# Moving the first normalisations of three groups to GpSimd in a two-stage transformer block on one core

## The chip, the cores and the metric

The kernel runs on one core of a Trainium2 chip. The number that counts is the device time of one launch in microseconds (us). The engines of the core, each with its own in-order stream of instructions, are PE (TensorE, the matrix engine; PEld is its loading of weights), DVE (VectorE), ACT (ScalarE), POOL (GpSimd) and SP (SyncE, which here issues nearly all transfers). An engine waits for others by semaphores, and everything that stands behind a waiting instruction on the same engine waits with it.

## The reference

The input x has 2048 rows of 512 channels, in bf16. Two residual steps follow each other; both are modulated by a vector c:

```python
mod = (_silu(c) @ w_mod).reshape(c.shape[0], 6, 1, -1)    # sa, ca, ga, sb, cb, gb
h = _layernorm(x, axis=-1) * (1 + ca) + sa
x = x + ga * _A_ref(h, A_wqkv, A_wo)
h = _layernorm(x, axis=-1) * (1 + cb) + sb
x = x + gb * _B_ref(h, B_w_gate, B_w_up, B_w_down)
```

`_A_ref` is an attention with 32 heads of 16 channels. Every row looks at 8 rows only: itself and those 2, 4, ... 14 rows before it. `_B_ref` is a gated feed-forward: gelu(h @ w_gate) * (h @ w_up), 1792 wide, times w_down.

## The kernel before

The rows are worked on in four groups of 512 (group 0 to 3), each laid out as 4 chunks of 128 rows. For one group the steps are these, with the lines of the kernel before:

- LN1: mean and variance of every row (DVE, L430 and L431, and for some chunks ACT, L408 to L419), then the inverse root as a power of -1/2 on POOL (`rst`, L471), then the normalised rows xn, one instruction per chunk of 128x512 (`norm_x`, L448, on DVE).
- xn is transposed so that channels lie on the partitions. This is done by PE as 16 small matmuls with the identity matrix for the names in `BY_PE` (`transp`, L484), and by one transposing DMA from SP for the others (L490). Four instructions (128x512 each) then multiply by 1 + ca and add sa (`transp_ev`, L522, on ACT) and leave hT. Group 0 has a path of its own (`transp0`, L507, and L538 and L540), in two halves.
- q, k and v: 12 tiles of 4 matmuls (L593), each copied out of PSUM by ACT (L613, L615, L619). v goes through DRAM (L625) and is read back four times, shifted (L634).
- The logits: DVE multiplies q by 8 shifted copies of k, four instructions pq of 128x4096 (L654), and PE sums over channels (LTp, L668). The softmax is on DVE and ACT (L680 to L712). Its weights go back to rows by PE and ACT (group 0, L726 and L735) or through DRAM (L740, L748).
- DVE multiplies by the shifted v, four instructions pv of 128x4096 (L761), PE sums (o_ps, L775), ACT copies (oT, L786), PE multiplies by wo (x_ps, L796), DVE adds x (L805).
- LN2, its transposition, then the feed-forward (g_ps and u_ps L829, gelu L863, copy L870, product L881, y_ps L841 and L853) and the stores.

The modulation vectors are products of w_mod with silu(c). The first two (sa and ca) are needed before any hT: `ldwm01` loads their 1024 columns in two halves of 256 rows (L245), `mods` multiplies them (L349), and DVE adds the 1 (L355). The blocks 2 to 5 of w_mod are loaded by L238 into two buffers in turn, so the third of these loads waits until PE has used the first. Blocks 2 and 5 become ga and gb (gR, L369), which scale wo and w_down (L391, L386). Blocks 3 and 4 become sb and 1 + cb (modT, L306).

The order of the work is written out. Every step is a generator of operations, called a thread, and the list `ORDER` holds the number of the thread whose next operation is issued. An engine gets its instructions in the order in which they are issued. Threads 0 to 29 are constants, loads, modulation and warm-up matmuls; group g has the 26 threads from 30 + 26g on. Nothing is decided at run time: a late operand makes the engine wait, and it does not take other work meanwhile.

Of the kernel before, what the change touches and what calls it, by code (L numbers as in the profile page):

```python
# [9 lines left out]
ALU = mybir.AluOpType  # L10
# [96 lines left out]
def kernel(  # L107
# [14 lines left out]
    P = 128  # L122
# [27 lines left out]
    def T(k, shape, dt, name):  # L150
        return pools[k].tile(shape, dt, name=name, tag=k)
# [69 lines left out]
    def loads():  # L221
# [5 lines left out]
        def ldx(sg, c0=0, c1=CPS, q=nc.sync):  # L227
            def f():
                if ("x", sg) not in B:
                    B["x", sg] = T("x", [P, CPS, D], BF16, "x")  # L230
                q.dma_start(out=B["x", sg][:, c0:c1, :],  # L231
                            in_=A_x[0, sg * SG:(sg + 1) * SG, :].rearrange("(p c) d -> p c d", p=P)[:, c0:c1, :])
            return f
# [8 lines left out]
        def ldwm01(h):  # L242
            if h == 0:
                B["wm01"] = T("prod", [P, 4, 2 * D], BF16, "wm01")
            nc.sync.dma_start(out=B["wm01"][:, 2 * h:2 * h + 2, :],  # L245
                              in_=w_mod[2 * h * P:(2 * h + 2) * P, 0:2 * D].rearrange("(t p) n -> p t n", p=P))

        def ldc():
            nc.sync.dma_start(out=c4[:], in_=c.rearrange("o (t p) -> (o t) p", p=P))
# [24 lines left out]
        def act_q():  # L274
            yield Op("ACT", 0.46, ldx(0, 2, 4, nc.scalar), fire="x0.2", lat=mb(0.25), dma=True)
        qs = [act_q()]
        def head_q():
            yield Op("SP", 0.47, ldx(0, 0, 2), fire="x0.0", lat=mb(0.25))
            yield Op("SP", 0.45, ldc, fire="c", lat=0.0)
            for h in range(2):  # L280
                yield Op("SP", 0.5, lambda h=h: ldwm01(h), take=[] if h else [SL["prod"]], fire=f"wm01.{h}", lat=mb(0.5))
# [45 lines left out]
    def mods():  # L327
# [15 lines left out]
        for h in range(2):  # L343
            def f(h=h):
                if h == 0:
                    B["mp01"] = T("mm", [P, 8], F32, "modT_ps")
                for ch in range(8):
                    for kt in (2 * h, 2 * h + 1):
                        nc.tensor.matmul(B["mp01"][:, ch:ch + 1], lhsT=B["wm01"][:, kt, ch * P:(ch + 1) * P],  # L349
                                         rhs=scT[:, kt:kt + 1], start=(ch == 0 and kt == 0), stop=(ch == 7 and kt == 3))  # L350
            yield Op("PE", 0.43, f, after=[f"wm01.{h}", "scT", "w15"], take=[] if h else [SL["mm"]],
                     give=[SL["prod"]] if h else [], fire=f"mp01.{h}")
# [3 lines left out]
        yield Op("DVE", 0.1, f, after=["mp01.1", "ident"], give=[SL["mm"]], fire="mod01")  # L356
# [81 lines left out]

    def norm_x(key, src, ev, parts=((0, 4),)):
        aa, ab = ACT_CH.get(ev, (0, 0))  # L440
        dv = [c4 for c4 in range(CPS) if not aa <= c4 < ab]
        for c4 in range(CPS):
            def f(c4=c4):
                k = norm_tiles(ev)
                if c4 == 0:
                    B[key] = T("xn", [P, CPS, D], BF16, "xn")
                m, o = (k["mv"][:, c4, 0:1], ALU.subtract) if c4 in dv else (k["s"][:, 1, c4:c4 + 1], ALU.add)
                nc.vector.tensor_scalar(out=B[key][:, c4, :], in0=src()[:, c4, :], scalar1=m,  # L448
                                        scalar2=k["rstd"][:, c4:c4 + 1], op0=o, op1=ALU.mult)
            yield Op("DVE", 0.325, f, after=[f"{ev}.rs{max(a for a, b in parts if a <= c4)}"],  # L450
                     take=[SL["xn"]] if c4 == 0 else [], fire=f"{ev}.x{c4}")
# [44 lines left out]
    BY_PE = ("LN1.1", "LN1.2", "LN2.0")  # L496
# [15 lines left out]
    def transp_ev(key, dkey, dtag, sc, bi, ev, dep):  # L512
        pe = ev in BY_PE
        for dtp in range(2):
            for dd in range(2):
                dt = 2 * dtp + dd

                def f(dt=dt, dtp=dtp, dd=dd):
                    if pe and dt == 0:
                        B[dkey] = T(dtag, [P, CPS, DT, P], BF16, dtag)  # L520
                    o = B[dkey][:, :, dt, :]
                    nc.scalar.activation(out=o, in_=B[key, dtp][:, :, dd, :] if pe else o, func=ACT.Identity,  # L522
                                         scale=sc(dt), bias=bi(dt))
                yield Op("ACT", 0.67 if pe else 0.71, f, after=[f"{ev}.t{dtp}" if pe else f"{ev}.t"] + dep,
# [437 lines left out]
```

## Time and profile before

Three runs took 237.4, 238.49 and 238.78 us; the median is 238.49. The profiled execution took 238.96 us, of which the profile covers a span of 237.1 us.

| what | us |
|---|---|
| profiled execution / its span | 238.96 / 237.1 |
| PE busy | 230.0 |
| DVE busy | 170.2 |
| ACT busy | 154.0 |
| POOL busy | 12.5 |
| PE idle from 12 us to 30 us of the span | 0.69 |
| PE idle from 30 us to 234 us | 0.75 |

All times in the text are counted from the start of the span. A row of the timeline has the start, the duration, the engine, the line, the operation and the tiles. A row of the chain of waits has the start and the duration of a piece of the work that ended last. A row of the groups has the busy time of all instructions of a kind and the mean of one in ns.

### The profile page before, as it was taken

The page shows a single profiled execution, that of the slowest core. Times are in us where ns is not written, and L with a number is a line of the kernel's source. Part 1 is how long each engine was busy: PE and PEld are TensorE (multiplying, and loading weights), DVE is VectorE, ACT ScalarE, POOL GpSimd, SP SyncE. Part 2 cuts the span into 40 slices and gives each one's busy share as a digit, 9 for nine tenths or more (in the row PEclk, how much of TensorE's full clock was granted, in tenths as well). Part 3 has the DMA queues.
Part 4 walks back from the last instruction along what each step waited for, and adds up shares of the span by engine and source line. Part 5 has one row for each costly group of instructions (what it writes and reads, how often), then busy time and mean ns, then how long its engine had stood idle before and what let it go on. Part 6 is the DMA issues. An engine that isn't in the chain of part 4 may idle for free.

```text
span 237.1 us, 3691 instructions
## 1 busy us (share of the span) xinstructions
PE 230.0 (97%) x1389; PEld 109.3 (46%) x1401; DVE 170.2 (72%) x238; ACT 154.0 (65%) x290; POOL 12.5 (5%) x39
## 2 busy tenths in 40 slices
PE   7798999999999999999999999999999999999995
PEld 2554555544554444444444444444444444444443
DVE  3799998999997999999997998978622202322222
ACT  4699999889798766947557962262679740266400
POOL 2510101000100000100000001000100000000000
PEclk9999999999999999999999999999999999999999
DMA  5999799999987529644105853810030001100011
GB/s 158 376 308 283 191 199 252 321 302 298 198 198 204 179 58 199 107 82 124 42 0 118 154 140 62 113 44 22 19 73 0 0 0 47 44 0 0 0 47 44
DMA packets 33417, 29.68 MB, mean 125 GB/s; under 512 B 12792, under 2 KB 30712, under 8 KB 33400
## 3 DMA queue, kind: packets, MB, share of 16 engines
q1 hardware_dynamic: 33256, 29.19, 50.2%
q10 hardware_dynamic: 144, 0.26, 0.4%
q8 instruction: 11, 0.18, 0.3%
q14 instruction: 6, 0.05, 0.1%
HBM read 22.37 MB, written 4.98 MB: 115 GB/s over the span
## 4 chain that ended last, share of the span: by engine, by line
PE 86%; DMA 8%; SPq 3%; ACT 1%; issue 1%; DVE 0%
PE g_ps L829 21%; PE u_ps L829 20%; PE y_ps L841 19%; PE qkv_ps L593 11%; PE x_ps L796 6%; DMA wm<-in_w_mod_dram 5%; DMA hT<-xn 3%; PE LTp L668 3%; PE o_ps L775 2%; SPq L223 1%; PE y_ps L853 1%; ACT hT L522 1%; PE hTp L484 1%; SPq L231 1%; PE modT_ps L306 0%
## 5 line engine op out<-in xcount | busy, mean ns | idle before, releaser
L829 PE MATMUL g_ps<-h,Wg 128*128 128x512 bf16 x224 | 57.4, 379 | 0.0
L829 PE MATMUL u_ps<-h,Wu 128*128 128x512 bf16 x224 | 57.3, 379 | 0.0
L863 ACT ACTIVATE gl<-g_ps 128x512 bf16<-128x512 f32 x56 | 33.5, 598 | 27.0 <-PE g_ps L829 27.0
L841 PE MATMUL y_ps<-Wd,hht 128*128 128x512 bf16 x203 | 45.6, 379 | 0.5 <-issue 0.2
L881 DVE TENSOR_TENSOR hht<-gl,ub 128x512 bf16<-128x512 bf16 x56 | 23.0, 421 | 31.8 <-ACT ub L870 31.7
L593 PE MATMUL qkv_ps<-hT,wqkv 128*128 128x512 bf16 x184 | 41.8, 380 | 0.5 <-ACT kT L615 0.4
L870 ACT CAST ub<-u_ps 128x512 bf16<-128x512 f32 x56 | 32.8, 586 | 14.4 <-PE u_ps L829 14.4
L654 DVE TENSOR_TENSOR pq<-qT,kT 128x4096 bf16<-128x4096 bf16 x16 | 36.1, 2285 | 0.2
L761 DVE TENSOR_TENSOR pv<-PT,V 128x4096 bf16<-128x4096 bf16 x16 | 35.8, 2284 | 0.1
L829 PEld LDWEIGHTS <-Wu 128*128 128x128 bf16 x224 | 21.8, 98 | 26.7 <-issue 0.8
L829 PEld LDWEIGHTS <-Wg 128*128 128x128 bf16 x224 | 21.6, 98 | 27.1 <-issue 1.7
L841 PEld LDWEIGHTS <-hht 128*128 128x128 bf16 x210 | 20.5, 98 | 25.0 <-issue 0.4
L593 PEld LDWEIGHTS <-wqkv 128*128 128x128 bf16 x184 | 20.2, 114 | 19.9 <-issue 2.8
L888 DVE TENSOR_TENSOR ot<-y_ps,x 128x512 bf16<-128x512 f32 x15 | 10.2, 689 | 20.1 <-PE y_ps L841 18.8
L471 POOL TENSOR_TENSOR rstd<-rstd,neghalf 128x4 f32<-128x4 f32 (+1 forms) x9 | 8.7, 966 | 154.8 <-DVE rstd L465 83.8
L522 ACT ACTIVATE h<-h,modT,scl 128x512 bf16<-128x512 bf16 x12 | 9.0, 805 | 11.8 <-DMA h<-xn 11.8
L796 PE MATMUL x_ps<-woP,oT 128*128 128x512 bf16 x60 | 15.3, 379 | 0.2
L430 DVE BATCH_NORM_STATS2 st<-x 128x6 f32<-128x512 bf16 x18 | 12.3, 686 | 3.5 <-DMA x<-in_A_x_dram 3.1
L786 ACT CAST oT<-o_ps 128x512 bf16<-128x512 f32 x16 | 8.6, 585 | 3.6 <-PE o_ps L775 3.6
L805 DVE TENSOR_TENSOR x<-x_ps,x 128x512 bf16<-128x512 f32 x16 | 10.7, 677 | 0.3 <-PE x_ps L796 0.2
L408 ACT ACTIVATE gl<-x 128x512 bf16<-128x512 bf16 x14 | 8.7, 630 | 2.9 <-DVE x L805 2.0
L796 PEld LDWEIGHTS <-oT 128*128 128x128 bf16 x64 | 7.2, 114 | 6.9 <-issue 0.4
(83 smaller groups left out, 183.2 us busy)
## 6 DMA issues: line engine op xcount, KB each, us to landing
V<-vscr SPq DMA_DIRECT2D x12, 520.0 KB, 8.5
wm<-in_w_mod_dram SPq DMA_DIRECT2D x6, 512.0 KB, 6.7
vscr<-vT SPq DMA_DIRECT2D x4, 512.0 KB, 6.3
out_dram<-ot SPq DMA_DIRECT2D x15, 128.0 KB, 1.7
Wu<-in_B_w_up_dram SPq DMA_DIRECT2D x1, 1792.0 KB
Wg<-in_B_w_gate_dram SPq DMA_DIRECT2D x1, 1792.0 KB, 9.5
wqkv<-in_A_wqkv_dram SPq DMA_DIRECT2D x3, 512.0 KB, 9.2
x<-in_A_x_dram SPq DMA_DIRECT2D x3, 512.0 KB, 9.5
```

The lines of the kernel that those rows point to most:

```text
L430: nc.vector.bn_stats(out=st[:], in_=src()[:, c4, :])
L522: nc.scalar.activation(out=o, in_=B[key, dtp][:, :, dd, :] if pe else o, func=ACT.Identity, scale=sc(dt), bias=bi(dt))
L593: nc.tensor.matmul(ps[:], lhsT=wqkv[blk][:, dt, j::4], rhs=B["hT", sg][:, :, dt, :], start=(dt == 0), stop=(dt == DT - 1))
L654: nc.vector.tensor_tensor(out=pq[:], in0=_ap(B["qT", sg][:, j, :], [[0, W], [1, SG]]), in1=_ap(kT[:, j, sg * SG + 2:sg * SG + 2 + SG], [[2 ...
L761: nc.vector.tensor_tensor(out=t[:], in0=_ap(B["PT", sg][:, 0, :], [[SG, 2], [0, 4], [1, SG]]), in1=_ap(v[:, 0, j, :], [[8, 2], [4 * (SG + ...
L796: nc.tensor.matmul(ps[:], lhsT=B["oT", sg][:, j, c4::CPS], rhs=woP[:, j, :], start=(j == 0), stop=(j == 3))
L805: nc.vector.tensor_tensor(out=x[:, c4, :], in0=B["x1ps", sg, c4][:], in1=x[:, c4, :], op=ALU.add)
L829: nc.tensor.matmul(ps[:], lhsT=Wt[:, dt, ft * P:(ft + 1) * P], rhs=B["h2T", sg][:, :, dt, :], start=(dt == 0), stop=(dt == DT - 1))
L841: nc.tensor.matmul(ps[:], lhsT=B["hh", sg, ft][:, c4 * P:(c4 + 1) * P], rhs=B["Wd", ft // 4][:, ft % 4, :], start=(ft == 0), stop=(ft == F ...
L863: nc.scalar.activation(out=gl[:], in_=B["g", sg, ft][:], func=ACT.Gelu_apprx_tanh)
L870: nc.scalar.copy(out=ub[:], in_=B["u", sg, ft][:])
L881: nc.vector.tensor_tensor(out=hh[:], in0=B["gl", sg, ft][:], in1=B["ub", sg, ft][:], op=ALU.mult)
```

## The change

- The normalised rows of LN1 of groups 1, 2 and 3 (12 instructions of 128x512) are written by POOL and not by DVE (`X_POOL`).
- LN1 of group 2 is transposed by a DMA and no longer by PE; that of group 3 was already. Their scaling and shifting (8 instructions of 128x512) is done by POOL in place of ACT (`H_POOL`).
- The loads of sa and ca are one block of 512 columns each, ca first, so rows of 1 KB in place of 2 KB. The matmuls follow block by block.
- Both halves of the first x come from SP, and the small vector c from ACT's queue; before, the second half of x came from ACT's queue and c from SP.
- `ORDER` is a new list. On PE the mods of block 3 move into the q, k, v matmuls of group 0, block 2 stands between the two transpositions of group 1 and block 4 behind them. On SP the transposing DMA of group 2 stands between the store of group 0's v and its four loads back. On DVE all four products pq of group 1 stand ahead of the four pv of group 0; before, two of them stood behind.

```diff
 ORDER = [
-    0, 0, 23, 23, 23, 23, 23, 23, 23, 23, 23, 23, 23, 2, 32, 2, 1, 22, 32, 32, 32, 32, 32, 22, 30, 30, 30, 32,
...
+    23, 1, 22, 0, 0, 23, 23, 23, 23, 2, 32, 2, 32, 23, 23, 22, 22, 24, 32, 32, 2, 2, 23, 23, 23, 23, 3, 30, 30,
...
-        def ldwm01(h):
-            if h == 0:
-                B["wm01"] = T("prod", [P, 4, 2 * D], BF16, "wm01")
-            nc.sync.dma_start(out=B["wm01"][:, 2 * h:2 * h + 2, :],
-                              in_=w_mod[2 * h * P:(2 * h + 2) * P, 0:2 * D].rearrange("(t p) n -> p t n", p=P))
+        def ldwm01(b):
+            if "wm01" not in B:
+                B["wm01"] = T("prod", [P, 4, 2, D], BF16, "wm01")
+            nc.sync.dma_start(out=B["wm01"][:, :, b, :], in_=w_mod[:, b * D:(b + 1) * D].rearrange("(t p) n -> p t n", p=P))
 
         def ldc():
-            nc.sync.dma_start(out=c4[:], in_=c.rearrange("o (t p) -> (o t) p", p=P))
+            nc.scalar.dma_start(out=c4[:], in_=c.rearrange("o (t p) -> (o t) p", p=P))
...
-        def act_q():
-            yield Op("ACT", 0.46, ldx(0, 2, 4, nc.scalar), fire="x0.2", lat=mb(0.25), dma=True)
-        qs = [act_q()]
+        qs = [one("ACT", 0.45, ldc, fire="c", lat=0.0, dma=True)]
         def head_q():
-            yield Op("SP", 0.47, ldx(0, 0, 2), fire="x0.0", lat=mb(0.25))
-            yield Op("SP", 0.45, ldc, fire="c", lat=0.0)
-            for h in range(2):
-                yield Op("SP", 0.5, lambda h=h: ldwm01(h), take=[] if h else [SL["prod"]], fire=f"wm01.{h}", lat=mb(0.5))
+            for c0 in (0, 2):
+                yield Op("SP", 0.47, ldx(0, c0, c0 + 2), fire=f"x0.{c0}", lat=mb(0.25))
+            for b in (1, 0):
+                yield Op("SP", 0.5, lambda b=b: ldwm01(b), take=[SL["prod"]] if b else [], fire=f"wm{b}", lat=mb(0.5))
...
+    X_POOL = ('LN1.1', 'LN1.2', 'LN1.3')
+
     def norm_x(key, src, ev, parts=((0, 4),)):
         aa, ab = ACT_CH.get(ev, (0, 0))
         dv = [c4 for c4 in range(CPS) if not aa <= c4 < ab]
+        eng, ve, w = ("POOL", nc.gpsimd, 0.75) if ev in X_POOL else ("DVE", nc.vector, 0.325)
...
-                nc.vector.tensor_scalar(out=B[key][:, c4, :], in0=src()[:, c4, :], scalar1=m,
+                ve.tensor_scalar(out=B[key][:, c4, :], in0=src()[:, c4, :], scalar1=m,
                                         scalar2=k["rstd"][:, c4:c4 + 1], op0=o, op1=ALU.mult)
-            yield Op("DVE", 0.325, f, after=[f"{ev}.rs{max(a for a, b in parts if a <= c4)}"],
+            yield Op(eng, w, f, after=[f"{ev}.rs{max(a for a, b in parts if a <= c4)}"],
...
-    BY_PE = ("LN1.1", "LN1.2", "LN2.0")
+    BY_PE = ('LN1.1', 'LN2.0')
+
+    H_POOL = ('LN1.2', 'LN1.3')
...
-                    nc.scalar.activation(out=o, in_=B[key, dtp][:, :, dd, :] if pe else o, func=ACT.Identity,
-                                         scale=sc(dt), bias=bi(dt))
+                    if ev in H_POOL:
+                        nc.gpsimd.tensor_scalar(out=o, in0=o, scalar1=sc(dt), scalar2=bi(dt), op0=ALU.mult, op1=ALU.add)
+                    else:
+                        nc.scalar.activation(out=o, in_=B[key, dtp][:, :, dd, :] if pe else o, func=ACT.Identity,
+                                             scale=sc(dt), bias=bi(dt))
```

More of the change, by code (lines that the diff above doesn't have):

```diff
@@ L225, in loads, with ldx @@
         B["x", 0] = T("x", [P, CPS, D], BF16, "x")
-        def ldx(sg, c0=0, c1=CPS, q=nc.sync):
+        def ldx(sg, c0=0, c1=CPS):
             def f():
@@ L230, in f @@
                     B["x", sg] = T("x", [P, CPS, D], BF16, "x")
-                q.dma_start(out=B["x", sg][:, c0:c1, :],
+                nc.sync.dma_start(out=B["x", sg][:, c0:c1, :],
                             in_=A_x[0, sg * SG:(sg + 1) * SG, :].rearrange("(p c) d -> p c d", p=P)[:, c0:c1, :])
@@ L341, in mods, with f @@
                  act="exp", fire="pre")
-        for h in range(2):
-            def f(h=h):
-                if h == 0:
+        for b in (1, 0):
+            def f(b=b):
+                if b:
                     B["mp01"] = T("mm", [P, 8], F32, "modT_ps")
[L347 to L352, printed above, removed]
+                for ch in range(4):
+                    for kt in range(4):
+                        nc.tensor.matmul(B["mp01"][:, 4 * b + ch:4 * b + ch + 1],
+                                         lhsT=B["wm01"][:, kt, b, ch * P:(ch + 1) * P], rhs=scT[:, kt:kt + 1],
+                                         start=(kt == 0), stop=(kt == 3))
+            yield Op("PE", 0.43, f, after=[f"wm{b}", "scT", "w15"], take=[SL["mm"]] if b else [],
+                     give=[] if b else [SL["prod"]], fire=f"mp{b}")
         def f():
             nc.vector.tensor_tensor(out=mod01[:], in0=B["mp01"][:], in1=c01[:], op=ALU.add)
-        yield Op("DVE", 0.1, f, after=["mp01.1", "ident"], give=[SL["mm"]], fire="mod01")
+        yield Op("DVE", 0.1, f, after=["mp0", "ident"], give=[SL["mm"]], fire="mod01")
     def mods_g(k):
@@ L521, in f @@
                     o = B[dkey][:, :, dt, :]
-                    nc.scalar.activation(out=o, in_=B[key, dtp][:, :, dd, :] if pe else o, func=ACT.Identity,
-                                         scale=sc(dt), bias=bi(dt))
-                yield Op("ACT", 0.67 if pe else 0.71, f, after=[f"{ev}.t{dtp}" if pe else f"{ev}.t"] + dep,
+                    if ev in H_POOL:
[3 more added lines that the diff above has]
+                                             scale=sc(dt), bias=bi(dt))
+                yield Op("POOL" if ev in H_POOL else "ACT", 0.75 if ev in H_POOL else 0.67 if pe else 0.71, f, after=[f"{ev}.t{dtp}" if pe else f"{ev}.t"] + dep,
                          take=[SL[dtag]] if pe and dt == 0 else [],
```

68 rows, old and new, of the table ORDER are left out of this document.

## The prediction

> **What bounds the kernel now.** I read the page's shares first, then the busy time in stretches of 6 us, then the chain of waits, then the timeline around each step that moves.
>
> ```profile
> PE 230.0 (97%) x1389; PEld 109.3 (46%) x1401; DVE 170.2 (72%) x238; ACT 154.0 (65%) x290; POOL 12.5 (5%) x39
> 12.00:18.00 6.00, 5.83 (x30) 3.13 (x29) 5.66 (x12) 5.87 (x17) 1.03 (x1) 1.00 1.10 303
> 18.00:24.00 6.00, 5.48 (x56) 2.92 (x55) 5.94 (x7) 5.77 (x14) 0.00 (x0) 1.00 0.96 284
> 24.00:30.00 6.00, 6.00 (x76) 3.19 (x74) 5.90 (x10) 5.94 (x17) 1.01 (x1) 1.00 0.72 189
> 42.00:48.00 6.00, 6.00 (x35) 3.02 (x37) 6.00 (x5) 4.74 (x10) 0.00 (x0) 1.00 1.23 310
> ```
>
> After the span come length and then PE, PEld, DVE, ACT, POOL. PE has no gap from 24 us to the end, at full granted clock (1.00). It is the bound, and a change can gain only PE work, the 0.69 us idle from 12 to 30 us, or the head. But from 12 to 60 us DVE is as full as PE, and what it makes is used soon after:
>
> ```profile
> 19.54 0.41 PE gR_ps L369 x16
> 23.65 0.55 PE hTp L484 x8
> 25.18 0.93 PE modT_ps L306 x32
> 26.66 5.30 PE qkv_ps L593 x24
> 31.96 0.89 PE hTp L484 x16
> 42.64 7.33 DMA hT<-xn
> ```
>
> The transpositions of group 1 run at 22.5 to 24.2, its q, k, v from 26.66. The 0.89 us at 31.96 are group 2's transpositions, which go away. The last row is the transposing DMA of group 3: 7.33 us to landing.
>
> **The change, part by part.**
>
> *PE work.* 16 transpositions go: -0.89 us, the row above, on the bound. All else on PE stays.
>
> *Head.* SP issues x0.0, x0.2 and the two modulation loads at the same places; x0.2 starts 0.45 us later (SP's issue rows at 0.80 and 1.25), covered because DVE reaches that half only at 6.16, after chunks 0 and 1. ACT now makes scT first and its statistics some 0.3 us later (end 6.7); DVE asks for them at 7.16. The second modulation load lets PE go on at 8.89, 1.36 us after the first (7.53): 512 KB at 385 GB/s. The stretch from 6 to 12 us, with the 1 KB rows of wqkv in it, moved 379 GB/s, so 1 KB rows lose little; between nothing and a fifth of 1.36 (0.27) I take +0.1. Two warm-up matmuls now stand between the halves of group 0's transpositions; DVE's five copies of 0.34 cover most: +0.1. Head +0.2, with ends -0.1 and +0.6.
>
> *Price of a POOL instruction.* No row shows a 128x512 one. The selections of 128x32 (0.213) and 128x128 (0.295) give 0.85 ns an element, so one pass over 512 is 0.62; two passes, one for each of its two operations, are 1.03. I take 0.75, nearer the single pass, for one instruction reads once and writes once. The Trainium skill, page GPSIMD Engine Reference, section 3.1, gives 769 ns for a tight loop over 512 elements; by it the estimate would be the same within 0.1 us.
>
> *What POOL does beside DVE.* That matters more than the price:
>
> ```profile
> 7.22 0.72 DVE L448 TENSOR_SCALAR xn<-x,mv,rstd 128x512 bf16<-128x512 bf16 x2
> 7.39 0.80 POOL L471 TENSOR_TENSOR rstd<-rstd,neghalf 128x2 f32<-128x2 f32 x1 [0.34 <-DVE rstd L465]
> 143.66 0.42 DVE L881 TENSOR_TENSOR hht<-gl,ub 128x512 bf16<-128x512 bf16 x1
> 143.89 1.05 POOL L471 TENSOR_TENSOR rstd<-rstd,neghalf 128x4 f32<-128x4 f32 x1 [44.78 <-DVE rstd L460]
> ```
>
> The 128x2 power took 0.71 with DVE idle or on statistics, and 0.80 here. The 128x4 one took 1.01 at 27.01, 40.16 and 61.87, and 1.05 at 98.06, 143.89 and 167.52, each time beside a product of two SBUF tiles. The first selection, at 8.43 beside xn, took 0.273, not 0.213. Set against what was left of the DVE instruction: 0.24 left cost 0.09, 0.20 cost 0.06, 0.18 to 0.19 cost 0.04. All five are the remainder less 0.15, as if POOL prepared for 0.15 us and then waited for that DVE instruction to end. Statistics (0.57 left at 14.58) and subtractions out of PSUM cost it 0.02 at most. The second xn above, and the hht that followed at 167.62, ran at usual length, so DVE is not held for all of a power, which touches 2 or 4 elements. The new instructions touch 512.
>
> Now DVE's work at the new places is pq and pv, 2.285 us each, with two SBUF tiles. Ends: POOL waits for nothing (0.75 each), or each waits out a pq or pv (up to 2.28 more) and holds the next one for its 0.6 us of data. I take turns, because five rows follow it and none contradicts; one turn is 2.24 + 0.6 = 2.84. The Trainium skill, page SBUF — State Buffer, section "SBUF: two separate sides", says that GpSimd and a DVE instruction with two SBUF inputs share one port pair, which the first holds for its whole instruction. Strictly so, a turn is 3.0 and the sum about 1 us higher. The xn that ran on under a power speaks against the strict form; none of these rows shows a long POOL instruction.
>
> *Group 1.* The power ends at 15.6. pq runs 15.5 to 17.8, so xn comes at 18.4; statistics fill DVE to 19.25 and xn 2 falls in there (19.1); two more turns put xn 3 and 4 at 22.1 and 24.95. Before, DVE had them at 19.1 and PE used them at 22.5. PE has nothing else in line: its transpositions end 2.4 us later. Behind them stand LTp, gR, the second half and block 4's matmuls, then 24 LTp; q, k, v of group 1 start at 28.9 in place of 26.66: +2.25. Of SP: block 4's load now waits for block 3's matmuls (20.9, before 19.95) and then 5.2 us as before (19.95 to 25.16), so 26.1; hidden under the later transpositions. Were these on time, it would hold PE from 24.6 to 26.1, and q, k, v would start at 28.1, +1.45.
>
> *Group 2.* xn at 27.2 to 30.2, while DVE is on softmax out of PSUM: no turns. The transposing DMA goes out at 30.2 on a queue with little under way; the three later ones landed after 4.6: 34.8. POOL scales until 37.8. PE wants it at 28.9 + 10.4 (48 matmuls) + 1.0 = 40.3: hidden. If it took 7.3, scaling would meet pq. Behind this DMA (3.7 us of issue) wait the four loads of V; the last goes out at 36 to 37 (33.71 before) and lands 8.7 later, at 46.1: pv cannot start before.
>
> *Group 3.* Its power follows DVE's variance, 43.6. One xn falls behind pq (45.5), one before pv, two take turns: 51.9, DMA to 56.5, scaled by 60.5. The four pv, with two turns of 0.6 and V's landing, end at 48.4, 51.25, 54.1 and 56.4 (before: 51.4). PE reaches its first 16 o_ps at 49.7 and waits 1.55; the second 16 at 54.0 and waits 2.4; x_ps waits 0.25. Group 3's q, k, v start at 62.0, so the scaling is just hidden.
>
> *Freed.* 12 xn of 0.41 on DVE (4.9 us) and 8 scalings of 0.80 on ACT (6.4) go; neither bounds, and DVE's saving is eaten by turns. PE's 0.40 wait for ACT at 18.23 should go, since kT is copied before the statistics.
>
> **Sum.** From the start of group 1's q, k, v to the first g_ps PE has 39.97 us of work and 4.2 of new waits: 28.9 + 39.97 + 4.2 = 73.1, and 0.41 of gR is now left for later, against 68.55: +4.9 us, the 0.89 already off. With the head +5.1. After that no moved step is on POOL and PE's work is the same. The profiled execution took 238.96 (span 237.1 and 1.86 around it), 0.47 above the median of the runs: 238.96 + 5.1 - 0.47 = 243.6.
>
> **Rivals.**
>
> - *Faster: POOL hardly waits.* If 512 elements cost no more beside pq than the 0.04 to 0.09 seen, xn of group 1 is done at 18.9, group 3 is scaled by 53.5, before PE's 55.5. If block 4's load also lands before 25 us, 0.89 and 0.40 are gained: 237.2. For it: no row has a long POOL instruction beside a long DVE one. Against: the remainder rule above. It decides if xn of group 1 is done before 22.3.
> - *No change: POOL hardly waits, the load does.* Then +1.45 at 26.1, +0.2 head, less 0.89 and about 0.6 of idle time: 238.6. For it: block 4's load has 5.2 us to land from the release of its buffer.
> - *Slower still: group 2 is late.* At 7.33 us to landing (the row above) hT lands at 37.5, and its four scalings take turns with pq: 46.5 in place of 40.3. With group 3 pushed along, g_ps starts 9.2 us late: 248. Against: nothing large is queued in front of this DMA.
>
> **How the numbers follow.** Turns 0.56: 243.6, its own range 241.5 to 246 (POOL at 0.62 or at 1.03: seven turns by -0.13 and +0.28, and V's landing). Group 2 late, or POOL always losing to the next pq, 0.14: 248 and over. Hardly any wait 0.30: of that faster 0.13, no change 0.10, and slower by the load alone 0.07. Two executions of one kernel here differ by 0.5%, 1.2 us, so that is what can be told apart. Faster 0.13, within 0.5% 0.10, slower 0.77. The range 237.5 to 249 leaves out the better half of the fast case and the worst of the late one.
>
> **What would show it.** Right: POOL rows of xn for group 1 of unequal length, 0.75 where DVE is on statistics and 2 to 3 us beside pq; pq rows above 2.285; PE waiting at the transpositions for POOL, and at o_ps for DVE's pv. Wrong: xn rows all near 0.75 and PE waiting for the DMA of block 4, or for nothing. What would make it wrong most easily is the rule of turns, drawn from instructions of 0.42 us or less; then V's landing.

## The result and the profile after

Four runs of the changed kernel took 250.5, 252.01, 253.09 and 253.84 us, median 252.55; the kernel before took 238.63 beside it (median of 4). The ratio is 1.0559 with a 95% interval from 1.0511 to 1.0607: 13.9 us slower, where 5.1 had been forecast and where 249 was the upper end of the range. The direction was right, the size was not. Ratios and their intervals leave out executions that took over 1.5% more than the fastest of the same kernel; medians are of all. The profiled execution took 250.5 us with a span of 248.7, so its trace has to account for 11.6 us against the 237.1 of before.

From the page of the changed kernel: the shares of the engines, the granted clock in 40 slices of 6.2 us, and the group of POOL's new instruction in its subtracting form.

```profile
PE 232.5 (93%) x1373; PEld 109.8 (44%) x1385; DVE 167.8 (67%) x226; ACT 149.5 (60%) x282; POOL 48.8 (20%) x59
PEclk9889769999999999999999999999999999999999
L449 POOL TENSOR_SCALAR xn<-x,mv,rstd 128x512 bf16<-128x512 bf16 x5 | 16.6, 3333 | 0.2
```

POOL is busy for 36 us more, and its xn in this form took 3.3 us a piece, not 0.75. PE has 16 instructions less and yet 2.5 us more of busy time: part of its work ran at a lower granted clock. Busy time in stretches of 6 us shows where (after the length: PE, PEld, DVE, ACT, POOL, then the granted clock, DMA share and GB/s):

```profile
24.00:30.00 6.00, 1.04 (x8) 0.44 (x6) 3.54 (x2) 0.77 (x2) 6.00 (x2) 0.84 0.50 170
30.00:36.00 6.00, 5.87 (x77) 3.25 (x78) 0.40 (x2) 4.75 (x10) 5.90 (x5) 0.59 0.01 3
```

PE, which was full from 24 to 30 us, does 1.04 us of work there; then it works for 6 us at a clock of 0.59. The timeline of POOL, of DVE and of PE (start, duration, what, and in brackets the idle time before it with what ended it):

```profile
16.84 12.49 POOL L449 TENSOR_SCALAR xn<-x,mv,rstd 128x512 bf16<-128x512 bf16 x3
29.31 0.76 POOL L449 TENSOR_SCALAR xn<-x,sums,rstd 128x512 bf16<-128x512 bf16 x1
41.53 3.01 POOL L526 TENSOR_SCALAR hT<-hT,mod 128x512 bf16<-128x512 bf16 x4 [4.74 <-DMA hT<-xn]
49.05 3.00 POOL L472 TENSOR_TENSOR rstd<-rstd,neghalf 128x4 f32<-128x4 f32 x1 [4.50 <-DVE rstd L466]
52.15 9.29 POOL L449 TENSOR_SCALAR xn<-x,sums,rstd 128x512 bf16<-128x512 bf16 x4
...
20.85 6.69 DVE L660 TENSOR_TENSOR pq<-qT,kT 128x4096 bf16<-128x4096 bf16 x3
54.09 9.48 DVE L767 TENSOR_TENSOR pv<-PT,V 128x4096 bf16<-128x4096 bf16 x4 [2.93 <-DMA V<-vscr]
...
29.38 0.40 PE L485 MATMUL hTp<-ident,xn 128*128 128x128 bf16 x2 [4.73 <-POOL xn L449]
35.44 10.55 PE L599 MATMUL qkv_ps<-hT,wqkv 128*128 128x512 bf16 x48
...
58.81 0.62 PE L781 MATMUL o_ps<-pv,Msum 128*32 128x512 bf16 x8 [1.59 <-DVE pv L767]
63.63 0.61 PE L781 MATMUL o_ps<-pv,Msum 128*32 128x512 bf16 x8 [1.81 <-DVE pv L767]
68.61 6.21 PE L599 MATMUL qkv_ps<-hT,wqkv 128*128 128x512 bf16 x28
...
79.86 1.03 PE L835 MATMUL g_ps<-h,Wg 128*128 128x512 bf16 x4
```

The first three xn of group 1 take 12.49 us: 2.08, 2.79 and, in a row of its own,

```profile
21.68 7.64 POOL L449 TENSOR_SCALAR xn<-x,mv,rstd 128x512 bf16<-128x512 bf16 x1
```

This third xn began during the first of three pq in a row and was done 1.8 us after the last of them (27.54). The pq run at their usual 2.2 us from start to start: POOL waits, DVE does not. All four xn stand in the chain of waits, from 16.84 to 30.08.

In the kernel before, the timeline has q, k, v of group 1 at 26.59 (26.66 in the chain of waits, where the prediction reads it) and the first g_ps here:

```profile
68.39 1.03 PE L829 MATMUL g_ps<-h,Wg 128*128 128x512 bf16 x4
```

With that the 11.6 us of the span can be placed. q, k, v of group 1 begin at 35.44 in place of 26.59, 8.85 later: in this execution PE's first full tile of q is 2.24 late already (14.73, before 12.49), PE waited 4.73 + 0.35 for POOL, and the work behind the wait was stretched by the clock. From there to the first g_ps it is 44.42 us, 2.6 more than before (79.86 - 35.44, against 68.39 - 26.59): 1.59 and 1.81 of waiting for pv, less 0.7 of PE's work (busy 40.97 in place of 41.66: the 16 transpositions went, and 16 matmuls of gR stand later now). That is 11.5 of the 11.6; behind it nothing moved.

### The profile page after: what moved, and what is told of

Same layout as the page of the kernel before. It is cut to its first block, busy times and chain, and to the rows that moved or that the text cites. A ratio compares the mean times of both kernels' runs of the same rounds, so it can differ in the third digit from the quotient of the medians.

```text
span 248.7 us, 3664 instructions
## 1 busy us (share of the span) xinstructions
PE 232.5 (93%) x1373; PEld 109.8 (44%) x1385; DVE 167.8 (67%) x226; ACT 149.5 (60%) x282; POOL 48.8 (20%) x59
## 4 chain that ended last, share of the span: by engine, by line
PE 78%; DMA 9%; POOL 5%; DVE 4%; SPq 1%; ACT 1%; issue 1%; POOLq 0%
PE g_ps L835 20%; PE u_ps L835 20%; PE y_ps L847 18%; PE qkv_ps L599 6%; PE x_ps L802 6%; POOL xn L449 5%; DMA gscr<-gR 4%; DMA wm<-in_w_mod_dram 3%; PE LTp L674 3%; PE o_ps L781 3%; DVE pv L767 2%; DMA gB<-gscr 2%; PE y_ps L859 1%; PE hTp L485 1%; SPq L640 1%
## 5 line engine op out<-in xcount | busy, mean ns | idle before, releaser
L887 DVE TENSOR_TENSOR hht<-gl,ub 128x512 bf16<-128x512 bf16 x56 | 22.9, 422 | 30.5 <-ACT ub L876 30.4
L767 DVE TENSOR_TENSOR pv<-PT,V 128x4096 bf16<-128x4096 bf16 x16 | 36.5, 2322 | 4.5 <-DMA V<-vscr 2.9
L472 POOL TENSOR_TENSOR rstd<-rstd,neghalf 128x4 f32<-128x4 f32 (+1 forms) x9 | 10.8, 1205 | 122.7 <-DVE rstd L461 69.7
L449 POOL TENSOR_SCALAR xn<-x,mv,rstd 128x512 bf16<-128x512 bf16 x5 | 16.6, 3333 | 0.2
L802 PE MATMUL x_ps<-woP,oT 128*128 128x512 bf16 x60 | 14.8, 379 | 0.2
L781 PE MATMUL o_ps<-pv,Msum 128*32 128x512 bf16 x128 | 9.1, 382 | 3.4 <-DVE pv L767 3.4
```

The source lines that it names most:

```text
L449: ve.tensor_scalar(out=B[key][:, c4, :], in0=src()[:, c4, :], scalar1=m, scalar2=k["rstd"][:, c4:c4 + 1], op0=o, op1=ALU.mult)
L767: nc.vector.tensor_tensor(out=t[:], in0=_ap(B["PT", sg][:, 0, :], [[SG, 2], [0, 4], [1, SG]]), in1=_ap(v[:, 0, j, :], [[8, 2], [4 * (SG + ...
L781: nc.tensor.matmul(o_ps[H * i:H * i + H, :], lhsT=M2[:], rhs=B["pv", sg, j][:, t, i, :], start=(t == 0), stop=(t == 1), tile_position=(0, ...
L802: nc.tensor.matmul(ps[:], lhsT=B["oT", sg][:, j, c4::CPS], rhs=woP[:, j, :], start=(j == 0), stop=(j == 3))
L887: nc.vector.tensor_tensor(out=hh[:], in0=B["gl", sg, ft][:], in1=B["ub", sg, ft][:], op=ALU.mult)
```

## The experiments

The runs had the kernel before beside them on the same chip (medians of 238.3 to 238.8). "Product" is from here on a DVE instruction of 2.2 us that multiplies two SBUF tiles, a pq or a pv.

**What a POOL instruction costs, alone and beside products.** A kernel without the model's work: POOL subtracts or adds, with scalars that lie next to each other or in steps of two, alone and then beside six DVE instructions.

```diff
+        for k in range(3):
+            ts("sub_step2_", k, mv[:, k, 0:1], ALU.subtract)
...
+        for i in range(6):
+            nc.vector.tensor_tensor(out=r[i % 2][:], in0=a[:], in1=b[:], op=ALU.mult)
+        for k in range(4):
+            ts("add_b2b_", k, mean[:, k:k + 1], ALU.add)
```

> This kernel leaves all of the model's work out: it copies x to the output and puts 128x512 GpSimd tensor-scalar instructions beside runs of six DVE instructions of 128x4096. Alone: theory A (a GpSimd instruction waits until no DVE product of two SBUF tiles is under way, and a back-to-back run of them keeps it out) and theory B (DVE and GpSimd take turns at every instruction boundary, and the slow part is the subtracting form) both expect 0.77 us for the adding form and 2.07 for the subtracting one; open is whether the step of the scalar or the operation makes 2.07. Beside six products back to back (13.5 us): A expects one GpSimd instruction of 8 to 13 us and the rest at 0.77 after the run; B expects four of about 2.2 to 2.9 us each. With a small memset between the products both expect about 2.3 to 2.9 each. Beside one-tile DVE instructions of 128x4096: A as stated expects no wait, 0.77 each.

The timeline of POOL and DVE in this kernel (the row at 51.30 is a product of the run with memsets):

```profile
9.55 6.18 POOL L43 TENSOR_SCALAR sub_step<-x,mv,rstd 128x512 bf16<-128x512 bf16 x3 [9.10 <-DVE rstd L38]
21.88 2.26 POOL L43 TENSOR_SCALAR add_step<-x,mv,rstd 128x512 bf16<-128x512 bf16 x3
26.69 2.17 POOL L48 COPY h<-g 128x4 f32<-128x4 f32 x1 [0.27 <-DVE g L47]
28.85 13.44 POOL L43 TENSOR_SCALAR add_b2b<-x,mean,rstd 128x512 bf16<-128x512 bf16 x4
51.30 2.68 DVE L51 TENSOR_TENSOR r<-a,b 128x4096 bf16<-128x4096 bf16 x1
...
59.77 8.09 POOL L43 TENSOR_SCALAR add_ts<-x,mean,rstd 128x512 bf16<-128x512 bf16 x4
...
26.54 13.70 DVE L51 TENSOR_TENSOR r<-a,b 128x4096 bf16<-128x4096 bf16 x6
```

Three adding instructions take 2.26 us, three subtracting ones 6.18, with either step: 0.75 and 2.06 apiece, so it is the operation that sets the price. Beside six products the copy of 4 elements waits for the running one and is through at its end (2.17). The adding instructions of 512 elements behind it took 7.05, 4.91, 0.76 and 0.76: the first waited through the three products that it met and was in before the next, which is 0.4 us longer for it (2.69 in place of 2.28). The second waited through the two products that were left and was in when the run was over, and the last two came when DVE was idle. Subtracting instructions in their place took 8.36, 4.91, 2.07 and 2.07, and the product behind the first was again 2.69. With a tiny memset between the products it was the same (7.08 and 4.92, and the row of 2.68); but that moved the starts of the products apart by 0.01 us only (2.21 in place of 2.20), so a real pause was not tested here. Beside instructions of one SBUF tile there are turns: 2.96 and then 1.73 each. Of the two explanations put up beforehand, let in at every boundary and let in only after the run, neither is right: an instruction of 512 elements gets in before the run is over, but only after the third product.

**Group 1 alone.** In the kernel before, only the four xn of group 1 go to POOL.

```diff
-                nc.vector.tensor_scalar(out=B[key][:, c4, :], in0=src()[:, c4, :], scalar1=m,
+                ve = nc.gpsimd if ev == "LN1.1" else nc.vector
+                ve.tensor_scalar(out=B[key][:, c4, :], in0=src()[:, c4, :], scalar1=m,
```

> The kernel before with one part of the change alone: the four normalisations of group 1 on GpSimd. Theory A: the four products of group 0 now run back to back from 15.5 to 24.5 us, the first normalisation gets in after two or three of them, the rest come after 24.5 at 2.07, 2.07 and 0.77 us; PE waits at the transposition from 22.5 to about 29, part of it at a lowered clock afterwards: plus 6 to 8 us, 244.5 to 247. Turns at every boundary: done by about 26, plus 3 to 4 us.

245.71 us, ratio 1.0297 (1.0229 to 1.0366): 7 us, half of the whole loss, and inside the 244.5 to 247 that the first theory expected. From its timeline and its stretches of 6 us:

```profile
15.16 12.21 POOL L449 TENSOR_SCALAR xn<-x,mv,rstd 128x512 bf16<-128x512 bf16 x3
27.42 0.28 PE L485 MATMUL hTp<-ident,xn 128*128 128x128 bf16 x2 [3.00 <-POOL xn L449]
```

```profile
30.00:36.00 6.00, 6.00 (x66) 2.47 (x65) 1.66 (x3) 4.28 (x13) 0.00 (x0) 0.50 1.10 191
```

PE waits 5.25 in all (1.79, 3.00, 0.46), and then runs for 6 us at half its clock. This is the changed kernel's group 1, without anything else of the change.

**The head alone.** Only the loads of sa and ca in rows of 1 KB, with their matmuls block by block, in the kernel before:

```diff
-                              in_=w_mod[2 * h * P:(2 * h + 2) * P, 0:2 * D].rearrange("(t p) n -> p t n", p=P))
+            nc.sync.dma_start(out=B["wm01"][:, :, b, :], in_=w_mod[:, b * D:(b + 1) * D].rearrange("(t p) n -> p t n", p=P))
```

> The kernel before with one part of the change alone: the first two modulation blocks in 1 KB rows, scale first, and their matmuls block by block. Theory C: the second load lands up to 0.7 us later, PE stands idle longer ahead of it, the granted clock falls for some us, and the first full q tile starts at 13 to 14.7 instead of 12.49: plus 0.5 to 2 us. Theory A alone: within 0.5 us of the kernel before.

238.62 us, ratio 1.0013 (0.9975 to 1.0051): nothing. In the changed kernel the first full tile of q is 2.2 us late (14.73, before 12.49), at a granted clock of 0.63 from 10 to 14 us. That need not be the change's doing, for it differs between executions with either head: the old head also had 14.73, at a clock of 0.65 (the run with group 2 on POOL, further below), and the changed one also 11.80, at full clock (the run with nothing on POOL). Eight more warm-up matmuls were to raise the clock:

```diff
-    pl.spawn(warmup(13, 18))
+    pl.spawn(warmup(13, 26))
```

> The changed kernel with eight more warm-up matmuls on PE ahead of the first modulation matmuls, so that PE is busy until about 8.3 us. If the low clock of 10 to 16 us comes from PE standing idle there: the clock stays at 1.0, the first full q tile starts near 12.5 to 13 (14.73 in the profile of the changed kernel), and the time is 1 to 2 us under the changed kernel with less spread between runs; the wait at 24 to 30 us stays. If not: no change.

251.88 us, ratio 1.0558 (1.049 to 1.0626): as without them. The clock was full and the tile came at 13.08, but POOL's three xn took 13.44 and group 1's q, k, v began at 36.56. An earlier head gained nothing here: the pq came earlier as well, and already the second xn met the run of three (7.53), in the changed kernel the third.

**Group 2 alone.** In the kernel before, group 2 is transposed by DMA, in its old order otherwise; then with its xn and its scaling on POOL as well.

```diff
-    BY_PE = ("LN1.1", "LN1.2", "LN2.0")
+    BY_PE = ("LN1.1", "LN2.0")
```

> The kernel before, with one thing of the change: group 2 transposed by DMA and not by TensorE. Its xn stays on VectorE and its scaling on ScalarE, all other work in its old place; the DMA goes out right after group 2's xn, ahead of the store of V, and the four scalings stand just before group 3's statistics. Theory 1 (the DMA route costs nothing; what the change lost behind group 1 was lost to GpSimd and to the new order): xn is complete at about 31, the DMA lands at about 36, ScalarE scales from 38 to 41.5, TensorE asks at 39.6 less 0.9: about 0.9 us of TensorE work goes and up to 2 us of wait come, 237.5 to 240. Theory 2 (the DMA route costs by itself: V's store and loads come 3.7 us later behind it on the queue, and pv waits): pv starts 1 to 4 us late and the time is 240 to 243.

> The run with group 2 transposed by DMA, and group 2's xn and its scaling now on GpSimd. Theory 1 (GpSimd is harmless where no run of products of two SBUF tiles is beside it): xn takes 2.07 a piece in its subtracting form and 0.77 in its adding form, begins at about 27.5 and ends by 35, the DMA lands at about 39.5, scaling is done by 42.7, against TensorE's 38.7: 3 to 4 us later than in the old place, 241 to 243. Theory 2 (the place is what counts: VectorE has pv from 42.5 on and scaling falls beside it): scaling takes 5 to 9 us for four, TensorE waits 6 to 9 us, and the time is 245 or more.

242.18 us, ratio 1.0151 (1.0102 to 1.02), and 244.74, ratio 1.0249 (1.0199 to 1.0299). From the timeline of the first of the two:

```profile
31.72 6.42 SPq L491 DMA_TRANSPOSE hT<-xn  x1
...
41.06 0.38 PE L594 MATMUL qkv_ps<-hT,wqkv 128*128 128x512 bf16 x1 [1.20 <-ACT hT L523]
```

SP needed 6.42 us to issue the transposition, with the loads of V under way; in the changed kernel, on an empty queue, it needed 1.77. hT landed at 40.2, 4 us later than expected, PE waited for it, and the clock was 0.72 from 42 to 48 us: 0.89 us of PE work saved, 3.4 us lost on balance. With POOL on top, xn took 4.59 for the two subtracting pieces and 1.51 for the two adding ones and was complete at 35.9 in place of 31.6, and scaling took 3.73: 2.6 us more. DVE was on softmax there, and POOL paid its price and little else.

**Group 3 alone.** In the kernel before, only xn and scaling of group 3 go to POOL.

```diff
+                ve = nc.gpsimd if ev in ("LN1.3",) else nc.vector
...
+                    if ev in ("LN1.3",):
+                        nc.gpsimd.tensor_scalar(out=o, in0=o, scalar1=sc(dt), scalar2=bi(dt), op0=ALU.mult, op1=ALU.add)
```

> The kernel before, with group 3's xn and its scaling on GpSimd and nothing else. xn becomes possible at 41.2, when VectorE has pv in line (four products) and then pq (two). Theory 1 (let in only after two or three products): the first xn is done at about 46 to 48, the fourth by 50, the DMA lands at 54 to 55, scaling beside pq ends at 58 to 60; TensorE asks for it at 58.9, so 0 to 2 us are lost: 238.5 to 241. Theory 2 (let in at each boundary): xn ends at 49 as well, but each product is longer by 0.6, scaling is done by 57 and nothing is lost. Both leave little; if the time is above 242, GpSimd was kept out of the run of six products altogether.

254.4 us, ratio 1.0648 (1.0591 to 1.0706): dearer than the whole change, where 238.5 to 241 had been expected. The timeline of POOL, SP and PE:

```profile
42.38 15.55 POOL L449 TENSOR_SCALAR xn<-x,sums,rstd 128x512 bf16<-128x512 bf16 x4
...
57.96 1.65 SPq L491 DMA_TRANSPOSE hT<-xn  x1
59.66 1.29 SPq L238 DMA_DIRECT2D wm<-in_w_mod_dram  x1
...
65.31 0.62 PE L369 MATMUL gR_ps<-wm,scB 128*32 128x128 bf16 x16 [12.57 <-DMA wm<-in_w_mod_dram]
```

Here all four are adding instructions, of 0.77 when nothing is beside them, and still four take 15.55: one of 0.77 before the six products begin, one of 7.04 through the first three pv, one of 7.03 through the last pv and two pq, and the fourth when DVE is done. PE's wait of 12.57 ends with a load of w_mod, which stood behind the transposition on SP's queue. Was it the queue? The same kernel with that load ahead of the transposition:

```diff
-    44, 17, 45, 66, 112, 113, 113, 113, 113, 88, 88, 89, 44, 18, 45, 26,
+    44, 17, 45, 66, 18, 112, 113, 113, 113, 113, 88, 88, 89, 44, 45, 26,
```

> The run with group 3's xn and scaling on GpSimd alone, with one load moved: the fifth modulation block, which stood behind group 3's transposing DMA on SP's queue and for which TensorE waited 12.57, is now issued ahead of it. Theory 1 (the queue made that run dear: SP stood at the transposition until xn was complete at 57.9, and the load behind it came as late): the wait of 12.57 goes, TensorE runs on until it asks for group 3's hT at about 58.9, which is there at 65.5 (transposition at 58, landing at 62.5, scaling 3.0): a wait of 5 to 7 us and some low clock behind it, 245 to 248. Theory 2 (GpSimd's time makes it dear, whatever stands on the queue): no more than 2 us come back, 252 or more.

253.2 us, ratio 1.0598 (1.0514 to 1.0683), about one us back, which the two intervals don't tell apart. The wait of 12.57 went and this came, at the tiles behind it:

```profile
62.40 0.58 PE L598 MATMUL qkv_ps<-hT,wqkv 128*128 128x512 bf16 x1 [10.05 <-POOL hT L525]
```

So POOL's 15.55 us are what costs, and the queue only decides which of PE's waits shows it. The first theory had put PE's request for group 3 at 58.9; the kernel before makes its first tile of group 3 at 52.2, and so has no slack there.

**The changed kernel with adding instructions.** POOL adds in place of subtracting, so the normalised rows are not the reference's; all else stays.

```diff
-                m, o = (k["mv"][:, c4, 0:1], ALU.subtract) if c4 in dv else (k["s"][:, 1, c4:c4 + 1], ALU.add)
+                m, o = (k["mv"][:, c4, 0:1], ALU.add if ev in X_POOL else ALU.subtract) if c4 in dv else (k["s"][:, 1, c4:c4 + 1], ALU.add)
```

> The changed kernel, but GpSimd adds the mean where it should subtract it (its output is therefore another one); only the form of five instructions differs. Theory B (price): all four of group 1 are done by about 23 us, PE hardly waits, 5 us or more under the changed kernel. Theory A (kept out by the run of products): the first three take 0.77 to 1.5, the fourth waits from about 21 until the third product ends near 27.5; q, k, v of group 1 start 1 to 1.5 us earlier than 35.4, and the time is 1 to 2 us under the changed kernel.

249.3 us, ratio 1.031 (1.0253 to 1.0367). Its four runs differ (245.92, 246.89, 251.71 and 253.89), and the ratio rests on the lower two; against the 1.0559 of the changed kernel it puts the subtracting form at some 6 us; 1 to 2 had been expected if POOL is kept out, 5 or more if the price decides. From the timeline of the execution of 245.92:

```profile
19.91 4.99 POOL L449 TENSOR_SCALAR xn<-x,sums,rstd 128x512 bf16<-128x512 bf16 x1
35.66 9.40 POOL L526 TENSOR_SCALAR hT<-hT,mod 128x512 bf16<-128x512 bf16 x4 [4.63 <-DMA hT<-xn]
...
45.11 6.38 PE L599 MATMUL qkv_ps<-hT,wqkv 128*128 128x512 bf16 x21 [2.48 <-POOL hT L526]
```

The cheaper form lets the first three xn through early, the fourth is caught for 4.99, and group 1's q, k, v begin at 28.3 (in an execution whose first full tile of q, at 12.16, is 2.57 earlier than the changed kernel's). But now group 2 is early as well, and its scaling meets pq: 9.40 for four, with PE waiting 1.89 and 2.48. In the changed kernel that scaling took 3.01 because everything before it was late.

**Gaps between the products.** The changed kernel with a tiny memset behind each of group 0's first three pq.

```diff
+                if sg == 0 and j < 3:
+                    nc.vector.memset(junk[:], 0.0)
```

> The changed kernel with a memset of 128x4 on DVE after each of the first three products of group 0. Theory A: the third normalisation of group 1 gets in at the first gap, near 23, the fourth at the second, near 26.4 (30.07 in the changed kernel); PE's wait shrinks by 3 to 4 us and the time by 3 to 5. Theory B: the products' boundaries were open already, so nothing moves, within 0.5 us.

253.48 us, ratio 1.0478 (1.0391 to 1.0565), with runs from 248.98 to 257.36; the ratio rests on 248.98 and 251.85, and its interval overlaps that of the changed kernel. The profiled execution, of 255.1, had three xn in 13.88 and PE waits of 5.02, 1.66 and 0.36: the short instruction opened nothing, as in the kernel without the model's work.

**Parts of the change taken back.** First group 1's xn on DVE again; then nothing at all on POOL; then xn of groups 2 and 3 alone on POOL.

```diff
-    X_POOL = ('LN1.1', 'LN1.2', 'LN1.3')
+    X_POOL = ('LN1.2', 'LN1.3')
```

> The changed kernel with the four normalisations of group 1 back on DVE, at the same place of the order. Both theories: the PE wait of 5.1 us for GpSimd goes, and with it the low clock from 28 to 36 us (about 1.9 us); a wait of about 1.3 us for block 4's load takes a part of its place. q, k, v of group 1 start near 30 us (35.4 in the changed kernel, 26.6 before); the time is 5 us (4 to 8) under the changed kernel, still 6 to 9 above the kernel before.

248.99 us, ratio 1.0409 (1.0339 to 1.0479), 3.6 less than the changed kernel, where 4 to 8 had been expected. q, k, v of group 1 begin at 29.59, some 6 us earlier; then this stands in the timeline:

```profile
40.73 7.23 POOL L526 TENSOR_SCALAR hT<-hT,mod 128x512 bf16<-128x512 bf16 x4 [4.63 <-PE LTp L674]
...
45.75 0.59 PE L599 MATMUL qkv_ps<-hT,wqkv 128*128 128x512 bf16 x1 [4.63 <-POOL hT L526]
```

The scaling of group 2 falls beside pq again and takes 7.23, PE waits 4.63 in place of 4.73 one group earlier, and the clock is 0.68 to 0.75 from 42 to 54 us.

```diff
-    X_POOL = ('LN1.1', 'LN1.2', 'LN1.3')
+    X_POOL = ()
-    H_POOL = ('LN1.2', 'LN1.3')
+    H_POOL = ()
```

> The changed kernel with all its normalising back on DVE and its scaling on ACT; the two DMA transpositions, the 1 KB-row loads and the new order stay. If GpSimd being kept out by DVE's products is the cause (theory A): no PE wait for GpSimd; DVE now waits twice for the power (about 1 us each), so the products of group 0 end near 30 us and q, k, v of group 1 start near 30.5 (35.4 in the changed kernel, 26.6 before); time 242.5 to 247, 6 to 10 under the changed kernel. If the order, the loads and the DMA transpositions carry most of the loss (theory C): above 248.

255.85 us, ratio 1.0706 (1.065 to 1.0763): slower than the changed kernel, where 242.5 to 247 had been expected from POOL as the cause. One wait of its timeline:

```profile
68.10 9.67 PE L599 MATMUL qkv_ps<-hT,wqkv 128*128 128x512 bf16 x28 [4.78 <-ACT hT L528]
```

The order of the change has DVE's and ACT's instructions where they suit a kernel in which POOL does this work: group 3's xn stands behind pv and wo's scaling on DVE, its transposition goes out at 62.89, and PE waits.

```diff
-    X_POOL = ('LN1.1', 'LN1.2', 'LN1.3')
+    X_POOL = ('LN1.2', 'LN1.3')
-    H_POOL = ('LN1.2', 'LN1.3')
+    H_POOL = ()
```

> The changed kernel with group 1's xn back on VectorE and the scaling of groups 2 and 3 back on ScalarE; xn of groups 2 and 3 stays on GpSimd, the DMA route and the new order stay. Theory 1 (what is left of the loss is GpSimd beside products: group 1's xn and then group 2's scaling): the wait of 4.63 at group 2's q, k, v goes, and 243 to 246 is left, for xn of group 2 and 3 and for V's landing. Theory 2 (the DMA route in this order carries a loss of its own, as the run with nothing on GpSimd suggests): ScalarE, in the written order, reaches the scaling late, TensorE waits 1 to 5 us for hT at group 2 or 3, and the time is 247 or more.

256.58 us, ratio 1.0741 (1.0685 to 1.0797). ACT comes to group 2's scaling before hT has landed, holds the copies of k behind it, and PE waits for those:

```profile
40.13 8.79 PE L599 MATMUL qkv_ps<-hT,wqkv 128*128 128x512 bf16 x28 [5.26 <-ACT kT L621]
```

From these three nothing can be read on what the new order costs by itself, since each also breaks that order.

**A version to beat both.** Group 2 by DMA in the old order, and one copy out of PSUM ahead of three statistics on ACT, to save PE's wait of 0.40 at 18.23.

```diff
-    37, 37, 37, 37, 82, 84, 36, 36, 36, 82, 82, 82, 37, 37, 37,
+    37, 37, 37, 37, 82, 84, 36, 36, 36, 37, 82, 82, 82, 37, 37,
```

> The run with group 2 transposed by DMA, and one more shift in the written order: one copy out of PSUM of group 0 stands ahead of three statistics of group 2 on ScalarE, not behind them, which is to take TensorE's wait of 0.40 for ScalarE at 18.23. Meant as a version that could beat both kernels. If the DMA route is free and the wait goes: 0.9 to 1.3 us less than before, 237.3 to 237.8. If the moved statistics make group 2's xn late: no gain beside the run without the shift.

242.06 us, ratio 1.0142 (1.011 to 1.0173), as without the shift, though that wait went. No version that was run beats the kernel before.

## Why the prediction was right and wrong

**Right: the place and the kind.** POOL is held up beside pq and pv; PE waits at the transpositions of group 1 for POOL, and at o_ps for pv. The o_ps waits were forecast as 1.55 and 2.4 and measure 1.59 and 1.81 (in part by luck, see V's landing). Group 2's scaling (41.53 to 44.54, wanted at 46.91) and group 3's (65.93 to 68.94, wanted piece by piece from 68.61) are hidden, as forecast. Block 4's load is hidden, and 1 KB rows alone cost nothing that can be measured. A small step was wrong: PE's wait of 0.40 for ACT did not go, 0.33 of it stands at 21.26.

**Wrong: "each waits out a pq or pv", a turn of 2.84.** This is the step that failed. The remainder rule was drawn from instructions of 2 to 4 elements beside DVE instructions of about 0.4 us. For instructions so small it holds beside products of 2.28 as well: the copy of 4 elements without the model's work, 2.17, and the power at 49.05, 3.00, waited for the end of one product. An instruction of 512 elements doesn't take its turn at the next boundary. By turns, the third xn of group 1 would have been in at 23.1, the end of the pq that it met, and done near 25 (the second was done 1.95 after its pq); it was done at 29.32. Beside a run of products such instructions took 7.64, 7.04, 7.04, 7.03 and 7.05 (three products); 4.91 where the run ended after two. Some came sooner: two that began 0.05 us ahead of a run's first product were in after one (2.90 in the run with more warm-up, 2.92 in that with gaps), and the 4.99 with adding instructions ended after two with a third behind them. The forecast had noted that none of its rows showed a long POOL instruction beside a long DVE one, and took the rule all the same as likeliest. What came about is the rival that was given 0.14 together with a late group 2, "POOL always losing to the next pq", at 248 and over; though it lost two boundaries in a row, not all. The Trainium skill, page SBUF — State Buffer, section "SBUF: two separate sides", has the pair of ports go to whichever starts first, for its whole instruction: the runs agree that a product keeps POOL out to its end; that POOL would then hold the next product for its own whole instruction they don't show, since the product behind a POOL instruction is 0.4 us longer (2.69 against 2.28), not 0.75 or 2.06.

**Wrong: the price of 0.75 for all twelve.** The adding form takes 0.767 and the subtracting one, which five of the twelve have, 2.07. The subtracting form has a large share of the loss: in the run with adding instructions, some 6 us faster in its two lower executions, group 1 begins at 28.3 and not at 35.4, since the shorter form is also caught by fewer products (a part of that is the earlier head of the execution). The price alone is not the cause either: with adding instructions only, group 3's xn lose 16 us. "xn at 27.2 to 30.2" for group 2 became 31.17 to 36.79 by both errors.

**Missing: the granted clock.** The sum had each wait cost its length. After waits of about 5 us PE runs on at a lower granted clock: 0.55 from 30.4 to 35.4 here, 0.50 from 30 to 36 in the run with group 1 alone. An estimate of what that costs here: from the end of the last xn (30.07) to q, k, v it took 5.37 in place of the forecast's 3.95, so 1.4 us more; 5.0 us at 0.55 make 2.25 at most. The Trainium skill, page TensorE: Matmul & The Clock Gate, Part 1, has the clock fall to half after about 3.4 us of idleness; the traces agree with the half, and show it after waits of 1.79 and 3.00 with a little work between them.

**Mis-sized: V's landing.** 46.1 was forecast for the four loads behind group 2's transposition. DVE waited for V until 54.09. Most of that is group 2's late xn, which moved the transposition to 36.83; the rest is the last two loads, which went out only at 42.25, behind the store of the next group's v. The o_ps waits come out near the forecast only because PE was late by nearly as much, 6.5.

**The sum.** Forecast: 28.9 for group 1's q, k, v and 73.1 for the first g_ps; measured 35.44 and 79.86. From the one to the other it is 44.42 where 44.2 was forecast, but that is luck: PE was busy there for 40.97 and not 39.97 (the 41.66 of the kernel before, less 0.89 and 0.41, are 40.36), and waited 3.45 and not 4.2. The profiled execution is 6.4 us above the 244.1 that the sum gives for it (238.96 + 5.1), and the 6.5 by which group 1 is later than forecast are all of that: 5.1 because its last xn was done at 30.07 and not at 24.95, which is the failed turns, the price and whatever the late head of this execution gave (a head of +0.2 was forecast), and 1.4 for the clock. The median of the runs is 2 us above the profiled one, which leaves open how much a given execution loses.

**What stays open.** The parts taken alone in the old order add up to 7 + 6 + 16 = 29 us, the change loses 14: they overlap, since PE that waits for group 1 does not need to wait as long for group 3. What the new order is worth by itself wasn't separated, nor, in the 5.1 us, the turns from the price. Nor does a run show why POOL, as a rule, loses two boundaries and wins the third, and why it sometimes came sooner. That the products which it waits through keep their 2.28 us, and that only the next is longer (2.69), speaks for 512 elements that get in all at once.

## What to carry to other kernels

Before elementwise work is moved to GpSimd, look for runs of DVE instructions with two SBUF tiles at the new place: one of them costs an instruction its remainder, a run of them up to three whole products. Rows of 4 elements say nothing about 512: measure the instruction in its own form (here subtract against add) and beside the work that it will meet. And price a wait of the bounding matrix engine of several us above its length, because the clock that is granted behind it is lower.

## What the runs showed that was not expected

- On GpSimd, subtract-and-multiply over 128x512 in bf16 takes 2.07 us, add-and-multiply 0.767; the step of the scalar operand makes no difference (6.18 us for three in either case).
- Beside back-to-back products GpSimd's instruction of 512 elements ends, as a rule, after three of them (7.03 to 7.08 us) or with the run (4.91 and 4.92 after two); the next product is then 0.4 us longer, whether the instruction alone takes 0.767 or 2.07. A memset of 62 ns between the products does not let it in sooner. Beside one-tile DVE instructions it is in by turns, 1.73 us each after a first of 2.96.
- Issuing one transposing DMA of 512x512 took SP 1.77 us with the queue empty and 6.42 with the loads of V under way.
